# dV and the weight gradients stored from SyncE instead of GpSimd, in the backward pass of a decode layer

## The chip, the cores and the metric

The kernel runs on one core of a Trainium2 chip. The metric is the device time of one execution in microseconds (us), the median of several runs. A profile is one more execution under the hardware profiler; its span is the time from the first to the last event, 1712.4 us for the kernel before.

A core has five engines, each with an instruction stream of its own that is worked through in order: TensorE (PE; PEld is its weight load), VectorE (DVE), ScalarE (ACT), GpSimd (POOL) and SyncE (SP). Data moves between device memory and the on-chip buffer by DMA. An engine issues a transfer with one instruction and goes on; 16 DMA engines carry it. Which engine issued a transfer decides the queue it stands in: q1 is SyncE's, q10 ScalarE's, q0 GpSimd's.

## The reference

One token per sequence for four sequences, 32 heads of 128, a cache of 4096 keys and values per head; then a gated MLP. The function returns the output and the gradients of its inputs. What matters here:

```python
q = (layernorm(x) @ wq)                              # (4, 32, 1, 128)
scores = einsum("bhqd,bhkd->bhqk", q, k_cache) * 128 ** -0.5
p = softmax(scores)
o = einsum("bhqk,bhkd->bhqd", p, v_cache)
h = x + o.reshape(4, 1, 4096) @ wo
gate, up = layernorm(h) @ w1, layernorm(h) @ w3
h2 = h + (silu(gate) * up) @ w2
# outputs: h2, and the vjp for grad_out of x, k_cache, v_cache, wq, wo, w1, w3, w2
```

With one query, the gradients of the caches are outer products. For each of the 128 (sequence, head) pairs, dV[k, :] = p[k] * dO[:] and dK[k, :] = dS[k] * q[:], where dS = p * (dP - c) * scale, dP[k] = V[k, :] . dO, and c is one number per pair. So each pair reads 1 MB of K once, 1 MB of V twice (forward and backward), and writes 1 MB of dK and 1 MB of dV, all bf16. The weight gradients are outer products too, some 13 MB in all.

## The kernel before

The kernel has a forward part (0 to about 650 us), a short middle part with the MLP, and a backward part from about 700 us to the end. All large buffers are taken from 23 equal slots of 8 KB per partition, handed out and given back in the order of a queue:

```python
free = deque(range(NSLOT))              # NSLOT = 23
class Slot:
    def __init__(self, name, src=free):
        self.i = src.popleft()
        self.t = slotp.tile([P, SLOT], BF16, name=name, tag=f"slot{self.i}")
    def give(self):
        free.append(self.i)
```

`give` is bookkeeping while the program is built. When a slot is used again, the instruction that writes it waits on the chip until its last reader, a store for instance, has finished.

The backward part loads each head's V into a ring of seven slots, transposes it in place (TensorE to PSUM, ScalarE back), and stores two outer products per head. L770 is VectorE's multiply in `outer`, L781 the dV store, L797 the V load and L1201 the dK store:

```python
def V_T(s, ps, part=range(SJ // GW)):
    ...
    for g in part:                                          # 4 parts of 8 transposes
        pt = ps.tile([P, GW, P], BF16, tag="tps", name="pt_tps")
        for i in range(GW):
            nc.tensor.transpose(pt[:, i, :], v[:, g * GW + i, :], ident_b[:])     # L764
        nc.scalar.copy(out=v[:, g * GW:(g + 1) * GW, :], in_=pt[:])               # L765

def grad_V(s):
    b, h = bh_of(s)
    gv = Slot("gv")
    outer(gv.heads(), P2s.pop(s), reps["rdo", s // REP][:, s % REP, :])           # L770
    nc.gpsimd.dma_start(out=rows_of(out_3[b, h]), in_=gv.heads())                 # L781
    if s > 1:
        gv.give()
    else:
        first_gv.append(gv)

def load_V2(eng=nc.sync):
    s = nv["next"]
    if s < NH:
        V2s[s] = Slot("V2", vring if vring else free)
        eng.dma_start(out=V2s[s].heads(), in_=cache_head(A_v_cache, s))           # L797
        nv["next"] += 1

def grad_K(s):
    b, h = bh_of(s)
    gk = Slot("gk")
    outer(gk.heads(), dS2s[s // B][:, s % B], reps["rq", s // REP][:, s % REP, :])  # L770
    nc.sync.dma_start(out=rows_of(out_2[b, h]), in_=gk.heads())                   # L1201
    gk.give()
```

`front(s)` transposes one head's V, makes dP with matmuls whose stationary operand is a small zero-padded window `zd` that GpSimd fills, and after every fourth head ScalarE copies dP out (dPr) and TensorE transposes it (dPT). `group_dS` makes dS of four heads on VectorE. GpSimd also doubles p into pairs for the outer product:

```python
def dO_window(s):                                            # GpSimd, L1142
    nc.gpsimd.tensor_copy(out=zd[s % B][:, 32:132:67], in_=dOT_bf[:, s:s + 1].to_broadcast([P, 2]))
def P_pairs(s):                                              # GpSimd, L1147
    nc.gpsimd.tensor_copy(out=P2s[s][:], in_=P_all[:, s, :, None].to_broadcast([P, SJ, 2]))

for s in range(2):
    dO_window(s)
for s in range(L):                                           # L = 5, LV = 3, S0 = 21, O0 = 2
    load_ahead(s); P_pairs(s); front(s)
    if s < 2: first_gv[s].give()
    elif s < LV + 1: grad_V(s)
group_dS(0)
for s in range(NH):                                          # NH = 128
    load_ahead(s + L)                                        # V loads: load_V2(nc.scalar)
    if s % REP == 0 and s + REP < NH: replicate(s + REP)     # rows of dO and q, for 4 heads
    P_pairs(s + L)
    if s + L < NH: front(s + L)
    ...
    if s > 0 and s + LV < NH: grad_V(s + LV)
    grad_K(s)
    if s % B == B - 1 and s + 1 < NH: group_dS((s + 1) // B)
    if s >= S0: step("s", 3 if s < S0 + 15 else 2)           # side work: dq, dx, weight gradients
    elif s >= O0: step("o")
step("s", 400)
```

The first two dV stores stand in the middle part, before the four `zd` windows are cleared (L1138). The side work makes the weight gradients in slots of their own and stores each from GpSimd: dwq four of 1 MB (L1026), dw2 two and dw1, dw3 two each of 0.9 MB (L1069, L1085), dwo four of 1 MB (L1096). It also loads wq (four of 1 MB) and w2 (two of 0.9 MB) again from SyncE.

Of the kernel before, what the change touches and what calls it, by code (L numbers as in the profile page):

```python
# [24 lines left out]
def kernel(  # L25
# [22 lines left out]
    nc = tc.nc  # L48
    P = nc.NUM_PARTITIONS
# [8 lines left out]
    HD = H * Dh  # L58
# [25 lines left out]
    def bh_of(s):  # L84
        return s % B, s // B

    def rows_of(ap):
        return ap.rearrange("(p j) d -> p j d", p=P)
# [89 lines left out]
    def ones_window(col):  # L178
# [11 lines left out]
                          in_=rowg[:, None, :, None].to_broadcast([P, 4, 8, 4]))  # L190
# [308 lines left out]
    def load_w2():  # L499
        sl = two_slots("w2")  # L500
        for i in range(2):
            nc.sync.dma_start(out=sl[i].b(7 * D).rearrange("p (c j) -> p c j", c=7),
                              in_=B_w2.rearrange("(p c) j -> p c j", c=FC)[:, i * 7:(i + 1) * 7, :])
        return sl
# [264 lines left out]
    def outer(dst, col2, row):  # L769
        nc.vector.tensor_tensor(  # L770
            out=dst.rearrange("p j (r t) -> p j r t", t=2),
            in0=col2[:, :, None, :].to_broadcast([P, SJ, Dh // 2, 2]),
            in1=row.rearrange("p (r t) -> p r t", t=2)[:, None, :, :].to_broadcast([P, SJ, Dh // 2, 2]),
            op=ALU.mult,
        )

    def grad_V(s):
        b, h = bh_of(s)
        gv = Slot("gv")
        outer(gv.heads(), P2s.pop(s), reps["rdo", s // REP][:, s % REP, :])  # L780
        nc.gpsimd.dma_start(out=rows_of(out_3[b, h]), in_=gv.heads())  # L781
        if s > 1:
            gv.give()
        else:
            first_gv.append(gv)
# [14 lines left out]
    with ExitStack() as cm:  # L800
# [108 lines left out]
        for b0, b1 in ((0, 1), (1, B)):  # L909
            ps = psA.tile([P, B, Dh], FP32, tag="rT", name="rep_ps")  # L910
            for b in range(b0, b1):
                for jj in range(DC):
                    nc.tensor.matmul(ps[:, b, :], lhsT=dhT[:, jj, b:b + 1].to_broadcast([P, P]), rhs=wo_page(0)[:, 0, jj, :],
                                     start=(jj == 0), stop=(jj == DC - 1))
            if b0 == 0:
                nc.vector.tensor_copy(out=rep_bufs["rdo"][0][:, 0:1], in_=ps[:, 0:1])
                grad_V(0)
            else:
                nc.scalar.copy(out=rep_bufs["rdo"][0][:, b0:b1], in_=ps[:, b0:b1])
        dO_columns(0, 8, psC, "cols")  # L920
        mid_w["wo"][0].give()
        grad_V(1)
        V_T(0, psT, range(2, SJ // GW))
        dO_rows(0, 8, psA, "rT")


    with ExitStack() as c2:
# [9 lines left out]
        def grad_flush():  # L937
            if gu:
                dst, ps, n = gu.pop()
                nc.scalar.copy(out=dst, in_=ps[:, 0:n])  # L940


        def grad_unit(dst, lhsT, rhs):
            n = rhs.shape[-1]
            ps = psg.tile([P, 512], FP32, tag="gps", name="gps")
            nc.tensor.matmul(ps[:, 0:n], lhsT=lhsT, rhs=rhs, start=True, stop=True)  # L946
            grad_flush()
            gu.append((dst, ps, n))


        def side_work():
# [65 lines left out]
            for cc in range(DC):  # L1017
                if cc == DC - 2:
                    w2 = load_w2()
                st = Slot("gwq")  # L1020
                for n8 in range(HD // 512):
                    grad_unit(st.b(HD)[:, n8 * 512:(n8 + 1) * 512], xhat_bf[0:B, cc * P:(cc + 1) * P],
                              flat.b(HD)[0:B, n8 * 512:(n8 + 1) * 512])
                    yield
                grad_flush()
                nc.gpsimd.dma_start(out=out_4[cc * P:(cc + 1) * P, :], in_=st.b(HD))  # L1026
                st.give()
            flat.give()
            fs.give()
# [32 lines left out]
            for i in range(2):  # L1062
                st = Slot("gw2")
                hw = hh_rows[:, i * 7 * P:(i + 1) * 7 * P].rearrange("b (p k) -> b k p", k=7)
                for k in range(7):
                    grad_unit(st.b(7 * D)[:, k * D:(k + 1) * D], hw[:, k, :], gr_bf)
                    yield
                grad_flush()
                nc.gpsimd.dma_start(out=out_8[i * 7 * P:(i + 1) * 7 * P, :].rearrange("(p c) j -> p c j", c=7),  # L1069
                                  in_=st.b(7 * D).rearrange("p (c j) -> p c j", c=7))  # L1070
                st.give()
            oflat = Slot("oflat")
# [2 lines left out]
            for (rows, out_ap) in ((dg_rows, out_6), (du_rows, out_7)):  # L1075
                for i in range(2):
                    st = Slot("gw13")
                    nw = hhat_bf[0:B, i * 2 * P:(i + 1) * 2 * P].rearrange("b (p k) -> b k p", k=2)
                    for k in range(2):
                        for (f0_, w_) in f_chunks:  # L1080
                            grad_unit(st.b(2 * F)[:, k * F + f0_:k * F + f0_ + w_],
                                      nw[:, k, :], rows[:, f0_:f0_ + w_])
                            yield
                    grad_flush()
                    nc.gpsimd.dma_start(out=out_ap[i * 2 * P:(i + 1) * 2 * P, :].rearrange("(p c) f -> p c f", c=2),  # L1085
                                      in_=st.b(2 * F).rearrange("p (c f) -> p c f", c=2))
                    st.give()
            r1.give()
            for h0 in range(0, H, 8):
                st = Slot("gwo")  # L1090
                ow = oflat.b(HD)[0:B, h0 * P:(h0 + 8) * P].rearrange("b (p k) -> b k p", k=8)
                for k in range(8):
                    grad_unit(st.b(8 * D)[:, k * D:(k + 1) * D], ow[:, k, :], dh_bf)
                    yield
                grad_flush()
                nc.gpsimd.dma_start(out=out_5[h0 * P:(h0 + 8) * P, :].rearrange("(p k) j -> p k j", k=8),  # L1096
                                  in_=st.b(8 * D).rearrange("p (k j) -> p k j", k=8))
                st.give()
            oflat.give()
            r2.give()  # L1100

        units["s"] = side_work()


# [113 lines left out]
        for s in range(L):  # L1218
            load_ahead(s)
            P_pairs(s)  # L1220
            front(s)
            if s < 2:
                first_gv[s].give()
            elif s < LV + 1:
                grad_V(s)
# [51 lines left out]
```

## Time and profile before

| | |
|---|---|
| time, median of 3 runs | 1716.86 us (1714.01 to 1718.6) |
| span of the profiled run | 1712.4 us |
| HBM read, written | 422.59 MB, 282.34 MB |
| mean rate over the span | 413 GB/s |
| busy: PE, DVE, ACT, POOL | 74%, 72%, 57%, 28% |

How to read it. The page gives busy time by engine, and then the span in 40 equal slices: a digit is the busy share of a slice in tenths, and two rows below give the busy share of the 16 DMA engines and the GB/s that they moved. A row of a DMA queue gives its packets, its MB and the time of its packets as a share of 16 engines' span. A row of a group of instructions reads: line, engine, operation, output <- input, count, then busy us and mean ns of one, then the idle time of the engine just before them and what ended most of it. A row of the waits reads: who waited, for whom, us in total, number of times, the longest. A row of a stretch reads: the stretch, its length, busy us and count for PE, PEld, DVE, ACT and POOL, then TensorE's granted clock, the DMA share and GB/s. A row of DMA issues gives output <- input, the issuing engine, count, size and the median us from issue to landing.

### The profile page before, as it was taken

To read this page: it belongs to the slowest core of one execution; us is meant where nothing else is said; L and a number is where in the kernel's file an instruction comes from. 1 tells how busy PE (TensorE), PEld (TensorE's weight loads), DVE (VectorE), ACT (ScalarE), POOL (GpSimd) and SP (SyncE) were. 2 spreads that over 40 slices of the span, in tenths; PEclk is the share of its full clock that TensorE was granted. 3 is DMA by queue.
4 is the path that set the end of the run, shared out by engine and by line. 5 is a ranking of instruction groups with operands and counts; after the bars stand their busy time and mean duration, and the time that the engine had idled before them with its cause. 6 is when DMAs were issued, how large, how long until landed. Compare 5 with 4: busy or idle time off the path is not lost. (4 is left out here: it accounts for less than half of the span.)

```text
span 1712.4 us, 38306 instructions
## 1 busy us (share of the span) xinstructions
PE 1259.2 (74%) x16180; PEld 930.6 (54%) x16180; DVE 1229.2 (72%) x1294; ACT 969.7 (57%) x1502; POOL 474.7 (28%) x822
## 2 busy tenths in 40 slices
PE   5889888888888888776788986675657656656660
PEld 4767677677677666644556764443334433333330
DVE  5989999989998996466667548475546465656584
ACT  3556445444544444676655466675766656666660
POOL 1211232223222321122333245353223231211140
PEclk8999999999999999898776579887896788887885
DMA  9999999999999999799999999999999999999997
GB/s 401 424 424 424 424 424 424 424 420 424 419 424 407 420 407 401 307 385 423 425 425 426 426 365 422 425 424 425 425 426 426 424 417 418 424 425 423 425 424 299
DMA packets 101740, 707.49 MB, mean 413 GB/s; under 512 B 11052, under 2 KB 15288, under 8 KB 17600
## 3 DMA queue, kind: packets, MB, share of 16 engines
q1 hardware_dynamic: 63568, 432.04, 60.5%
q0 software_dynamic: 20864, 148.22, 20.7%
q10 hardware_dynamic: 17136, 124.79, 17.6%
q8 instruction: 127, 2.08, 0.5%
q14 instruction: 45, 0.37, 0.1%
HBM read 422.59 MB, written 282.34 MB: 412 GB/s over the span
## 5 line engine op out<-in xcount | busy, mean ns | idle before, releaser
L765 ACT COPY V<-pt_tps 128x1024 bf16<-128x1024 bf16 x512 | 490.8, 1025 | 155.3 <-PE pt_tps L764 115.9
L764 PE MATMUL pt_tps<-ident_b,V 128*128 128x128 bf16 x4096 | 359.0, 249 | 206.5 <-ACT V L765 201.4
L764 PEld LDWEIGHTS <-V 128*128 128x128 bf16 x4096 | 306.8, 114 | 269.1 <-issue 257.8
L770 DVE TENSOR_TENSOR gv<-P,reps 128x4096 bf16<-128x4096 bf16 x125 | 287.0, 2296 | 129.4 <-DMA out_dram<-gv 123.6
L770 DVE TENSOR_TENSOR gk<-dS,reps 128x4096 bf16<-128x4096 bf16 x128 | 292.5, 2287 | 112.7 <-DMA out_dram<-gv 80.4
L421 DVE TENSOR_TENSOR PK<-Kn,PK 128x4096 bf16<-128x4096 bf16 x128 | 292.4, 2284 | 26.4 <-POOL PK L417 26.0
L436 PE MATMUL M_ps<-PK,Vn 128*128 128x130 bf16 x4096 | 285.8, 222 | 32.3 <-DMA Vn<-in_A_v_cache_dram 31.9
L436 PEld LDWEIGHTS <-Vn 128*128 128x128 bf16 x4096 | 253.8, 99 | 52.0 <-DMA Vn<-in_A_v_cache_dram 43.0
L328 DVE STREAM_TRANSPOSE KT<-Kn 128x512 f32<-128x512 f32 (+1 forms) x321 | 250.7, 797 | 0.3 <-issue 0.2
L1177 PE MATMUL dP_ps<-V,zd 128*32 128x512 bf16 x1024 | 185.3, 452 | 72.3 <-ACT V L765 61.8
L323 ACT COPY KT<-pt_tps 128x1024 bf16<-128x1024 bf16 x128 | 129.5, 1012 | 185.3 <-PE pt_tps L322 150.7
L781 POOL DMA_DIRECT2D out_dram<-gv x128 | 68.4, 535 | 498.9 <-DVE gv L770 470.6
L417 POOL COPY PK<-P_all 128x64 bf16<-128x64 bf16 x128 | 32.6, 255 | 415.5 <-ACT P_all L411 412.4
L334 POOL TENSOR_TENSOR W<-qrep,wmask 128x128 bf16<-128x128 bf16 x128 | 122.9, 960 | 83.0 <-PE S_ps L354 68.3
L1147 POOL COPY P<-P_all 128x64 bf16<-128x64 bf16 x127 | 137.3, 1081 | 0.0
L1177 PEld LDWEIGHTS <-zd 128*32 128x32 bf16 x1024 | 37.3, 96 | 161.8 <-issue 140.3
L1142 POOL COPY zd<-dOT_bf 128x2 bf16<-128x2 bf16 x128 | 90.5, 708 | 71.5 <-PE dP_ps L1177 71.5
L1191 DVE TENSOR_SCALAR dPr<-dPT_ps,c_rep 128x32 f32<-128x32 f32 x128 | 23.2, 242 | 119.1 <-PE dPT_ps L1159 118.9
L1131 ACT CAST reps<-rep_ps 128x512 bf16<-128x512 f32 x62 | 36.4, 586 | 121.0 <-DVE gk L770 86.5
L411 ACT COPY P_all<-pt_P 32x64 bf16<-32x64 bf16 x256 | 52.1, 203 | 53.8 <-PE pt_P L407 51.6
L322 PE MATMUL pt_tps<-ident_b,Kn 128*128 128x128 bf16 x1024 | 81.0, 224 | 0.0
L446 PE MATMUL kP_ps<-PK,onesw 128*32 128x512 bf16 x1024 | 79.9, 389 | 0.0
(244 smaller groups left out, 1358.7 us busy)
## 6 DMA issues: line engine op xcount, KB each, us to landing
Kn<-in_A_k_cache_dram SPq DMA_DIRECT2D x128, 1024.0 KB, 15.3
Vn<-in_A_v_cache_dram SPq DMA_DIRECT2D x128, 1024.0 KB, 15.6
out_dram<-gv POOLq DMA_DIRECT2D x128, 1024.0 KB, 29.7
out_dram<-gk SPq DMA_DIRECT2D x128, 1024.0 KB, 13.9
V<-in_A_v_cache_dram ACTq DMA_DIRECT2D x119, 1024.0 KB, 14.8
V<-in_A_v_cache_dram SPq DMA_DIRECT2D x9, 1024.0 KB, 18.3
wq<-in_A_wq_dram SPq DMA_DIRECT2D x8, 1024.0 KB, 18.3
out_dram<-gw POOLq DMA_DIRECT2D x6, 896.0 KB, 42.0
```

Source lines behind the costliest of these rows:

```text
L322: nc.tensor.transpose(pt[:, i, :], Kn[:, c * GW + i, :], ident_b[:])
L323: nc.scalar.copy(out=KT[:, c * GW:(c + 1) * GW, :], in_=pt[:])
L328: nc.vector.transpose(out=KT[:, c * w_:(c + n) * w_], in_=Kn[:, c * w_:(c + n) * w_])
L334: nc.gpsimd.tensor_tensor(out=W[:, hl], in0=qrep[:, :, s:s + 1].to_broadcast([P, 4, 32]), in1=wmask[:, hl, None, :].to_broadcast([P, 4, 32 ...
L421: nc.vector.tensor_tensor(out=PK[:, :, 0:Dh].rearrange("p j (r t) -> p j r t", t=2), in0=Ks[s].heads().rearrange("p j (r t) -> p j r t", t=2),
L436: nc.tensor.matmul(hold["M"][:], lhsT=Vn[:, j, :], rhs=PK[:, j, :], start=(j == 0), stop=(j == SJ - 1))
L764: nc.tensor.transpose(pt[:, i, :], v[:, g * GW + i, :], ident_b[:])
L765: nc.scalar.copy(out=v[:, g * GW:(g + 1) * GW, :], in_=pt[:])
L770: nc.vector.tensor_tensor(out=dst.rearrange("p j (r t) -> p j r t", t=2), in0=col2[:, :, None, :].to_broadcast([P, SJ, Dh // 2, 2]), in1=r ...
L1142: nc.gpsimd.tensor_copy(out=zd[s % B][:, 32:132:67], in_=dOT_bf[:, s:s + 1].to_broadcast([P, 2]))
L1147: nc.gpsimd.tensor_copy(out=P2s[s][:], in_=P_all[:, s, :, None].to_broadcast([P, SJ, 2]))
L1177: nc.tensor.matmul(rows["acc"][32 * c:32 * (c + 1), :], lhsT=zq_window(zd[hl], 2 * hl + u), rhs=VT[:, j0:j0 + 4, :], start=(hl == 0 and u ...
```

## The change

All large stores that GpSimd issued are issued by SyncE: the 128 stores of dV and the 14 of the weight gradients. The dK stores were SyncE's and the V loads of the backward loop ScalarE's already, so with the change no large transfer is left to GpSimd; it keeps a few of some kilobytes. The purpose is to free GpSimd of issuing and of waiting for VectorE, and to have the stores in a queue of the hardware's own descriptor generation. Five lines change, each in the same way:

```diff
@@ grad_V @@
         outer(gv.heads(), P2s.pop(s), reps["rdo", s // REP][:, s % REP, :])
-        nc.gpsimd.dma_start(out=rows_of(out_3[b, h]), in_=gv.heads())
+        nc.sync.dma_start(out=rows_of(out_3[b, h]), in_=gv.heads())
@@ side_work: dwq @@
-                nc.gpsimd.dma_start(out=out_4[cc * P:(cc + 1) * P, :], in_=st.b(HD))
+                nc.sync.dma_start(out=out_4[cc * P:(cc + 1) * P, :], in_=st.b(HD))
@@ side_work: dw2 @@
-                nc.gpsimd.dma_start(out=out_8[i * 7 * P:(i + 1) * 7 * P, :].rearrange(...),
+                nc.sync.dma_start(out=out_8[i * 7 * P:(i + 1) * 7 * P, :].rearrange(...),
@@ side_work: dw1, dw3 @@
-                    nc.gpsimd.dma_start(out=out_ap[i * 2 * P:(i + 1) * 2 * P, :].rearrange(...),
+                    nc.sync.dma_start(out=out_ap[i * 2 * P:(i + 1) * 2 * P, :].rearrange(...),
@@ side_work: dwo @@
-                nc.gpsimd.dma_start(out=out_5[h0 * P:(h0 + 8) * P, :].rearrange(...),
+                nc.sync.dma_start(out=out_5[h0 * P:(h0 + 8) * P, :].rearrange(...),
```

The order of instructions on TensorE, VectorE and ScalarE stays as it was. SyncE's stream gets the dV stores between the dK stores, in the order in which VectorE makes them. In the built program, the large transfers of SyncE and ScalarE wait on semaphores of one set, those of GpSimd on semaphores of another:

```
before, SyncE:   dK store   [waits DMAHW2, DVE]      after, SyncE:   dV store   [waits DMAHW0, DVE]
                 dK store   [waits DMAHW6, DVE]                      dK store   [waits DMAHW1, DVE]
before, GpSimd:  dV store   [waits DMASW5, DVE]                      dV store   [waits DMAHW2, DVE]
before, ScalarE: V load     [waits DMAHW4, ACT]      after, ScalarE: V load     [waits DMAHW0, ACT]
```

More of the change, by code (lines that the diff above doesn't have):

```diff
@@ L1068, in side_work @@
                 grad_flush()
-                nc.gpsimd.dma_start(out=out_8[i * 7 * P:(i + 1) * 7 * P, :].rearrange("(p c) j -> p c j", c=7),
+                nc.sync.dma_start(out=out_8[i * 7 * P:(i + 1) * 7 * P, :].rearrange("(p c) j -> p c j", c=7),
                                   in_=st.b(7 * D).rearrange("p (c j) -> p c j", c=7))
@@ L1084, in side_work @@
                     grad_flush()
-                    nc.gpsimd.dma_start(out=out_ap[i * 2 * P:(i + 1) * 2 * P, :].rearrange("(p c) f -> p c f", c=2),
+                    nc.sync.dma_start(out=out_ap[i * 2 * P:(i + 1) * 2 * P, :].rearrange("(p c) f -> p c f", c=2),
                                       in_=st.b(2 * F).rearrange("p (c f) -> p c f", c=2))
@@ L1095, in side_work @@
                 grad_flush()
-                nc.gpsimd.dma_start(out=out_5[h0 * P:(h0 + 8) * P, :].rearrange("(p k) j -> p k j", k=8),
+                nc.sync.dma_start(out=out_5[h0 * P:(h0 + 8) * P, :].rearrange("(p k) j -> p k j", k=8),
                                   in_=st.b(8 * D).rearrange("p (k j) -> p k j", k=8))
```

## The prediction

> **What bounds the kernel now.** I read the page first, its row of slices and its queues. Four rows carry the reading: the busy share of the DMA engines and their GB/s in 40 slices of 42.8 us, and the three queues that carry the large transfers (q1 is SyncE's, q10 ScalarE's, q0 GpSimd's).
>
> ```profile
> DMA  9999999999999999799999999999999999999997
> GB/s 401 424 424 424 424 424 424 424 420 424 419 424 407 420 407 401 307 385 423 425 425 426 426 365 422 425 424 425 425 426 426 424 417 418 424 425 423 425 424 299
> ...
> q1 hardware_dynamic: 63568, 432.04, 60.5%
> q0 software_dynamic: 20864, 148.22, 20.7%
> q10 hardware_dynamic: 17136, 124.79, 17.6%
> ```
>
> The reader is to see that nearly every slice stands at one rate, 424 GB/s, whichever queues are at work: slices 1 to 7 hold loads of SyncE alone, the later ones loads and stores of three queues. The kernel is bound by its DMA. Then I cut the span where the slices dip, and asked for busy time and DMA of each stretch (the last two columns are the DMA share and GB/s):
>
> ```profile
> 700.00:740.00 40.00, 27.11 (x317) 17.84 (x315) 21.07 (x17) 26.82 (x31) 10.56 (x29) 0.91 0.73 275
> 740.00:1000.00 260.00, 209.51 (x1915) 154.34 (x1910) 159.09 (x119) 155.02 (x177) 76.98 (x101) 0.75 1.01 425
> 1000.00:1020.00 20.00, 14.38 (x160) 10.13 (x158) 18.31 (x14) 14.30 (x17) 16.02 (x14) 0.89 0.81 299
> 1020.00:1695.00 675.00, 418.89 (x4040) 265.00 (x4037) 418.50 (x298) 429.24 (x533) 201.82 (x274) 0.82 1.01 424
> 1695.00:1712.40 17.40, 0.00 (x0) 0.00 (x0) 0.00 (x0) 0.00 (x0) 0.00 (x0) 0.50 0.27 116
> ```
>
> All 707.49 MB at 424 GB/s would take 1668.6 us. The span is 1712.4, so 43.8 us are lost. Each stretch loses its length times (1 - its GB/s / 424): 700 to 740 us 14.1, 1000 to 1020 us 5.9, the end 12.6. What is left, 11.2 us, lies before 700 us, where the change moves nothing: the first dV store is issued at 702.4. So the change can reach 14.1 + 5.9 + 12.6 = 32.6 us at the very most.
>
> Last I read the waits and the issues, to see who waits for the stores that move:
>
> ```profile
> L781 POOL DMA_DIRECT2D out_dram<-gv x128 | 68.4, 535 | 498.9 <-DVE gv L770 470.6
> ...
> out_dram<-gv POOLq DMA_DIRECT2D x128, 1024.0 KB, 29.7
> out_dram<-gk SPq DMA_DIRECT2D x128, 1024.0 KB, 13.9
> V<-in_A_v_cache_dram ACTq DMA_DIRECT2D x119, 1024.0 KB, 14.8
> ```
>
> ```profile
> DVE gv L770 <- DMA out_dram<-gv: 123.6, 42, 6.8
> DVE dPr L1191 <- PE dPT_ps L1159: 118.9, 11, 22.9
> DVE gk L770 <- DMA out_dram<-gv: 80.4, 30, 9.5
> ```
>
> A dV store lands 29.7 us after its issue, a dK store after 13.9, and VectorE waits 123.6 + 80.4 = 204 us for slots that a dV store still holds. That looks like 204 us to gain. It isn't: during these waits the DMA engines are full (the 424 GB/s rows), so VectorE waits for bytes, not for a slow queue.
>
> **What the Trainium skill says.** "DMA: Bandwidth & Descriptors", section "Issuing engines are not separate DMA queues": transfers of any issuing engine run on the same 16 DMA engines and interleave. The trace agrees: share divided by MB is 0.140% for q1, 0.140% for q0, 0.141% for q10, so a byte costs the same on each. The same page, "Queues, rings and completion order": a DMA engine takes turns among the queues that hold work. The trace fits; three queues that all want the engines divide them evenly, and GpSimd's, with more stores pending, has the longest time to landing. Its section "Latency and other measured facts" gives about 1 us to the first byte for GpSimd's path and 0.6 us for the other; the trace shows no such gain, for the shortest dV landing is 4.2 us and the shortest dK landing 4.7. "SBUF — State Buffer", section "SBUF: two separate sides", warns that VectorE can lock GpSimd out while it writes descriptors and leave the DMA engines idle. No full stretch here shows it: they are at 424 with or without q0.
>
> **The change part by part.**
>
> Bytes: none added or removed. At equal cost per byte the 1668.6 us stay: 0 us.
>
> GpSimd's issues: 128 + 14 large stores at 0.53 us, some 76 us of an engine that is 28% busy. It also stands still 470.6 us behind VectorE in these issues, and its small copies (zd, P) stand behind them in program order. Where DMA is full that costs nothing. In the dip at 700 to 740 us it does: no store can flow until the chain of V transposes for the first five heads is through, and the first dP matmul waits 3.52 us, until 706.48, for a zd copy. GpSimd had stood at the issue of the second dV store until 704.94. Without it the cast (0.22 us) can start when the c_ps matmuls end, near 703.0, then the four memsets (0.67) and the zd copy (0.2): 704.1 or so. Gain about 2.2 us, on the path.
>
> SyncE's issues: 142 more at 0.33 us, 47 us on an engine that does nothing else. 0 us.
>
> Semaphores: the built program shows something that the diff doesn't. Large transfers of SyncE and ScalarE take eight semaphores in turn, in program order, and each waits for the transfer that had it eight before; GpSimd's have eight of their own. In the kernel before, dV stores stood outside; now a head has three transfers in one ring of eight (V load, dV store, dK store), and the side work's join them. A V load then waits for the dV store of about three heads earlier, and that wait is in ScalarE's own instruction stream, ahead of its copies. In flight before, between 1020 and 1640 us: dV 77 x 36.2 / 620 = 4.5, dK 77 x 13.7 / 620 = 1.7, V 78 x 14.6 / 620 = 1.8, side work about 1.1, together 9 MB (an estimate, from median landings). After, at most 8, or 8 x 2.47 = 19.8 us of work (1.0486 MB at 424 GB/s is 2.47 us). That still fills the engines, if nobody holds the ring longer. Per head the DMA needs 3 x 2.47 = 7.4 us, ScalarE 429.24 / 78 = 5.5, VectorE 418.5 / 80 = 5.2, so each can follow. When the dV store lands on which ScalarE waited, about seven stores are still to go, some 17 us; ScalarE and TensorE need about 5 us to the next dS and VectorE 3.5 to the next store, 8.5 in all. The ring is closed with some 8 us to spare: 0 us in the mean. In the dip at 1000 us, where ScalarE needs 12 us for a head (its V loads are issued at 991.7 and 1003.5), a held ring may cost about 2 us more.
>
> The end: VectorE stops at 1688.9, all 16 engines are busy to about 1696, and then the rows fall to 27 GB/s, a sixteenth of 424, for some 8 us: one DMA engine finishes alone. Fewer stores in flight and one order for all may shorten this by 2 or 3 us; I count 2.
>
> Sum: -2.2 (first dip) + 2 (second) - 2 (end) = -2.2 us from 1716.86. As the slot order also becomes the landing order, which may trim small waits, I set 1713.
>
> **The rivals.**
>
> First rival, GpSimd's queue was the brake: its descriptors cost the DMA engines time, or make the one engine fall behind that ends last. For it: dV landings of 29.7 us against 13.9, and the lone engine at the end. Against it: equal cost per byte, and the same 424 in stretches without q0. If the lone engine is its doing, 8 us go at the end: about 1703. It can't exceed the 32.6 us.
>
> Second rival, the ring of eight becomes a new wait: ScalarE stands at a V load, TensorE and VectorE stall behind it, and the DMA engines run dry in places that are full today because nine transfers and a separate dV queue bridge a stall. For it: VectorE already has stalls of up to 22.9 us at dPr, and ScalarE already waits for dK stores ahead of its V loads:
>
> ```profile
> ACT V L765 <- DMA out_dram<-gk: 17.9, 7, 5.8
> ```
>
> Against it: the 8 us to spare above, and that slots bound the stores in flight before semaphores do at 740 to 1000 us. If one group of four heads in three among the last 20 groups lost 3 us, that is 20 us: 1735.
>
> Third rival, the changed order on SyncE: weight loads now stand behind dV stores too. But a slot of a load comes from the oldest store, which lands first now; I give it nothing.
>
> **Range and chances.** The hidden case (nothing but a few us) has about two thirds, around 1713; the first rival a sixth, down to 1703; the ring a sixth, up to 1735 and thinly beyond. Range 1700 to 1735. Faster by over 2% means under 1682.5, a gain of 34 us, more than all the idle time that the change can reach: 0.01. Slower by over 2% means over 1751, a ring that runs dry often: 0.09. Within 2%: 0.90.
>
> **What would show it.** Right: about 424 GB/s in all slices from 18 to 38 but the dip; the first dP matmul near 704 us; dV and dK landings alike near 20 us; VectorE's wait for stores moved from one name to the other and about as long in total; GpSimd's 470 us gone and nothing gained by it. First rival: share per MB falls, or the last 17 us shrink to under 10. Second: new slices under 410 between 740 and 1690 us, with ScalarE waiting for gv or gk stores ahead of its V loads by far more than today's 18 us. I'd be wrong most likely by a stall that I took for bridged.

## The result and the profile after

The changed kernel takes 1728.3 us (median of four runs, 1727.0 to 1731.4) against 1716.7: a ratio of 1.0071, 95% interval 1.0051 to 1.0091. It is slower by 0.7%, 15 us above the 1713 that was predicted, inside the range: a loss of 12 us where a gain of 4 was forecast. The profiled span went from 1712.4 to 1727.6 us, by 15.2; the ledger below is of these two executions.

First the page of the kernel after: the DMA share and GB/s in 40 slices, the packets, and the two queues that are left for large transfers.

```profile
DMA  9999999999999999799999989999999999999998
GB/s 402 423 425 423 425 423 425 423 425 423 415 423 409 423 406 401 280 425 420 418 419 369 395 341 418 423 416 418 417 423 420 414 412 421 420 413 414 413 425 354
DMA packets 101741, 707.50 MB, mean 410 GB/s; under 512 B 11052, under 2 KB 15288, under 8 KB 17600
...
q1 hardware_dynamic: 84016, 580.16, 80.8%
q10 hardware_dynamic: 17136, 124.79, 17.9%
```

The bytes are the same. Counted from 0, slices 0 to 15 are as before but for a few GB/s, and 16 and 17 are the first dip, which the wider slices cut elsewhere. From slice 18 on, two things have changed. Slices 21 to 23 are low (369, 395, 341, where one slice dipped before). And most slices after them stand at 412 to 421 where most stood at 422 to 426, although their digit is a 9 as before. The second sign is easy to overlook: a DMA engine that is full isn't yet at its rate.

The stretches of the backward part, cut where the slices change (columns: busy us of TensorE, its weight loads, VectorE, ScalarE and GpSimd; the share of its full clock that TensorE was granted, DMA share, GB/s). The kernel after:

```profile
700.00:740.00 40.00, 28.26 (x330) 18.68 (x329) 21.44 (x17) 27.27 (x32) 11.79 (x24) 0.91 0.76 288
740.00:900.00 160.00, 112.79 (x1151) 78.41 (x1151) 102.17 (x76) 102.33 (x119) 26.94 (x45) 0.82 1.01 421
900.00:1020.00 120.00, 106.44 (x782) 85.07 (x781) 62.20 (x49) 55.49 (x64) 29.85 (x27) 0.61 0.91 365
1020.00:1710.00 690.00, 445.01 (x4160) 287.26 (x4158) 427.04 (x304) 442.40 (x545) 285.47 (x180) 0.79 1.01 418
1710.00:1727.60 17.60, 0.00 (x0) 0.00 (x0) 2.16 (x1) 0.00 (x0) 0.00 (x0) 0.50 0.59 249
```

And the kernel before, in the two of these that the prediction didn't cut so:

```profile
740.00:900.00 160.00, 119.13 (x1238) 82.31 (x1234) 106.27 (x84) 107.44 (x125) 49.08 (x70) 0.83 1.01 425
900.00:1020.00 120.00, 104.75 (x837) 82.16 (x835) 71.13 (x49) 61.88 (x70) 43.92 (x45) 0.66 0.98 404
```

The prediction's measure, length times (1 - GB/s / 424), gives the loss of each stretch:

| stretch | lost before, us | lost after, us | difference |
|---|---|---|---|
| 700 to 740 | 14.1 | 12.8 | -1.3 |
| 740 to 900 | -0.4 | 1.1 | +1.5 |
| 900 to 1020 | 5.7 | 16.7 | +11.0 |
| 1020 to the end of the full part | 0 | 9.8 | +9.8 |
| the end | 12.6 | 7.3 | -5.3 |

The sum is 15.7, against 15.2 in the span. The same difference splits in a second way. Share of all queues times span is the time that packets took on a mean DMA engine: before 99.4% of 1712.4, or 1702.1 us; after 99.3% of 1727.6, or 1715.5. So 13.4 us are longer packets for the same bytes, and only some 2 are more idle time. The idle time hides two opposite moves: in 900 to 1020 the share fell from 0.98 to 0.91 (about 8 us more), and at the two ends idle time fell by about 6. I call 1702.1 and 1715.5 the packet time from here on. It is a sum of printed shares, each rounded to 0.1%, so it is good to about 3 us; the packet records added up one by one give 1699.4 and 1713.3 us, 13.9 apart.

The large groups that the change touches, in the page of the kernel after (GpSimd's copies of P first; then the issues, with the median us from issue to landing):

```profile
L1147 POOL COPY P<-P_all 128x64 bf16<-128x64 bf16 x127 | 218.6, 1721 | 346.2 <-DVE gv L770 345.8
...
out_dram<-gv SPq DMA_DIRECT2D x128, 1024.0 KB, 18.7
out_dram<-gk SPq DMA_DIRECT2D x128, 1024.0 KB, 18.8
V<-in_A_v_cache_dram ACTq DMA_DIRECT2D x119, 1024.0 KB, 10.2
```

dV and dK stores now land alike, near the 20 us of a ring of eight. V loads land in 10.2 us, earlier than the 14.8 of before. GpSimd's wait in the issues is gone, and most of it has only moved to its next copy. Last the waits (total us, times, longest):

```profile
DVE dPr L1191 <- PE dPT_ps L1159: 332.4, 28, 18.6
...
ACT V L765 <- DMA out_dram<-gv: 101.4, 22, 7.8
...
ACT V L765 <- DMA out_dram<-gk: 22.6, 3, 13.7
...
DVE gv L770 <- DMA out_dram<-gv: 10.7, 10, 2.3
...
DVE gk L770 <- DMA out_dram<-gv: 5.9, 5, 2.4
```

The wait for stores has changed engine. VectorE waited 204 us for slots that dV stores held; now 16.6 us (10.7 + 5.9), and 39.1 for stores of both kinds (22.5 us behind dK stores). ScalarE waited 17.9 us for stores ahead of its V loads; now 124.0 (101.4 + 22.6). The view books this wait at L765, the copy that comes next in ScalarE's stream. Behind ScalarE stand TensorE's V transposes, dP and dPT, and behind those VectorE, which now waits 332.4 us at dPr instead of 118.9.

### The profile page after: what moved, and what is told of

It is laid out like the page before. It is cut to its first block, busy times and chain, and to the rows that moved or that the text cites. A ratio compares the mean times of both kernels' runs of the same rounds, so it can differ in the third digit from the quotient of the medians.

```text
span 1727.6 us, 38312 instructions
## 1 busy us (share of the span) xinstructions
PE 1280.1 (74%) x16180; PEld 951.4 (55%) x16180; DVE 1227.7 (71%) x1294; ACT 971.6 (56%) x1502; POOL 523.6 (30%) x680
## 3 DMA queue, kind: packets, MB, share of 16 engines
q1 hardware_dynamic: 84016, 580.16, 80.8%
q10 hardware_dynamic: 17136, 124.79, 17.9%
## 5 line engine op out<-in xcount | busy, mean ns | idle before, releaser
L765 ACT COPY V<-pt_tps 128x1024 bf16<-128x1024 bf16 x512 | 491.5, 1024 | 248.5 <-PE pt_tps L764 117.5
L764 PE MATMUL pt_tps<-ident_b,V 128*128 128x128 bf16 x4096 | 374.2, 255 | 206.5 <-ACT V L765 201.2
L764 PEld LDWEIGHTS <-V 128*128 128x128 bf16 x4096 | 320.5, 117 | 266.1 <-issue 256.7
L1147 POOL COPY P<-P_all 128x64 bf16<-128x64 bf16 x127 | 218.6, 1721 | 346.2 <-DVE gv L770 345.8
L770 DVE TENSOR_TENSOR gv<-P,reps 128x4096 bf16<-128x4096 bf16 x125 | 287.9, 2303 | 21.1 <-DMA out_dram<-gv 10.7
L1191 DVE TENSOR_SCALAR dPr<-dPT_ps,c_rep 128x32 f32<-128x32 f32 x128 | 23.3, 245 | 332.4 <-PE dPT_ps L1159 332.4
L1142 POOL COPY zd<-dOT_bf 128x2 bf16<-128x2 bf16 x128 | 132.1, 1032 | 186.2 <-PE dP_ps L1177 186.2
L322 PEld LDWEIGHTS <-Kn 128*128 128x128 bf16 x1024 | 61.8, 99 | 25.7 <-issue 25.6
L400 ACT ACTIVATE Pn<-E,rl 128x1024 bf16<-128x1024 f32 x64 | 73.7, 1152 | 3.2 <-DVE rl L397 3.2
## 6 DMA issues: line engine op xcount, KB each, us to landing
out_dram<-gv SPq DMA_DIRECT2D x128, 1024.0 KB, 18.7
V<-in_A_v_cache_dram ACTq DMA_DIRECT2D x119, 1024.0 KB, 10.2
out_dram<-gw SPq DMA_DIRECT2D x6, 896.0 KB, 14.8
```

Source lines behind the costliest of these rows:

```text
L322: nc.tensor.transpose(pt[:, i, :], Kn[:, c * GW + i, :], ident_b[:])
L770: nc.vector.tensor_tensor(out=dst.rearrange("p j (r t) -> p j r t", t=2), in0=col2[:, :, None, :].to_broadcast([P, SJ, Dh // 2, 2]), in1=r ...
```

## The experiments

Two theories stood at the start. The **ring theory**: a V load waits in ScalarE's own stream for the store eight transfers earlier, the chain behind ScalarE stalls, and the DMA runs dry or out of step. The **queue theory**, a rival: what matters is which queues the bytes are in, and how they share the DMA engines, whatever ScalarE waits for. A third, that SyncE's long list of issues or the order of its loads costs something, stood beside them. All kernels compute the whole of the reference. Each ratio, with its 95% interval, is to the kernel before as it ran beside that kernel. There its median was 1714.3 to 1716.7 us, so medians of different experiments compare to about 2 us.

**dV alone** (the changed kernel, with the weight gradients back on GpSimd) and **weight gradients alone** (the kernel before, with these on SyncE):

```diff
# dv_only, against the kernel after: dwq, dw2, dw1 and dw3, dwo (dV stays on SyncE)
-                nc.sync.dma_start(out=out_4[cc * P:(cc + 1) * P, :], in_=st.b(HD))
+                nc.gpsimd.dma_start(out=out_4[cc * P:(cc + 1) * P, :], in_=st.b(HD))
# wgrads_only, against the kernel before: the same four lines the other way (dV stays on GpSimd)
```

> The changed kernel with the 14 weight-gradient stores put back on GpSimd; only the dV stores stay on SyncE. If the ring of eight semaphores with three transfers per head is the cause, nearly all of the loss stays: 1725 to 1729 us, ScalarE waiting some 100 us for dV stores ahead of its V loads. If the weight gradients in SyncE's stream are the cause (they wait for ScalarE's copies and hold dV and dK stores behind them), it falls back to 1715 to 1719.

> The kernel before with only the 14 weight-gradient stores moved to SyncE; dV stays on GpSimd. Ring of eight: two transfers per head and a few more, so no new waits: 1715 to 1719. Weight gradients as the cause: 1725 to 1729.

Measured: dV alone 1736.3 us, 1.0121 (1.0107 to 1.0136). Weight gradients alone 1721.3 us, 1.0038 (1.0025 to 1.0050). The dV stores are the larger part, but the two parts don't add: with dV on SyncE, moving the 14 others as well makes the kernel 8 us faster; with dV on GpSimd, the same move costs some 6.5 us. I have no cause for that. The second run holds a surprise for the ring theory, in its waits:

```profile
DVE dPr L1191 <- PE dPT_ps L1159: 292.6, 26, 23.7
...
ACT V L765 <- DMA out_dram<-gk: 124.1, 19, 16.6
```

ScalarE waits as long for its V loads as in the kernel after, and VectorE nearly as long at dPr, at half the cost in time.

**V loads elsewhere.** In the kernel after, the V loads of the backward loop are issued from GpSimd, or from SyncE, so that nothing in ScalarE's stream waits for a transfer of the ring:

```diff
-                load_V2(nc.scalar)
+                load_V2(nc.gpsimd)      # v_gpsimd, in both places;  nc.sync in v_sync
```

> The changed kernel with the V loads of the backward loop issued from GpSimd, so that stores (SyncE) and loads (GpSimd) have eight semaphores each and ScalarE issues nothing. Ring theory: ScalarE never waits for a store, no dry stretch but that of the kernel before, 1708 to 1718. If stores from SyncE's queue are slow in themselves, or if loads and stores simply pack worse in two queues than in three: 1725 to 1730. If GpSimd's loads come late because GpSimd stands behind its small copies: TensorE waits for V, over 1730.

> The changed kernel with the V loads of the backward loop on SyncE too: one queue for all large transfers, ScalarE issues none and waits for no store. The ring of eight stays, and its order. First theory (ScalarE's waits at the V loads cost the time): back to 1716 to 1721, the waits of ScalarE for stores gone. Second theory (a queue that starts again after a pause stretches the packets under way; the V queue does it over 100 times in the changed kernel): packets over 400 ns nearly vanish, DMA at 424 GB/s where it is busy. Rival (the ring itself lets the DMA run dry, whoever waits at it): 1728 or more, since a V load that waits for its slot now holds the stores behind it as well.

Measured: from GpSimd 1718.7 us, 1.0014 (1.0004 to 1.0025). Its dip stays:

```profile
900.00:1020.00 120.00, 106.30 (x789) 83.77 (x788) 65.61 (x46) 57.47 (x66) 30.65 (x43) 0.61 0.94 384
```

ScalarE has no wait for a store ahead of its V copies here, and VectorE waits only 80.9 us at dPr, yet the DMA share falls to 0.94. GpSimd stands some 500 us in front of its V loads instead. So the dry stretch doesn't need a wait in ScalarE's stream; more on it below.

From SyncE, with every large transfer of the backward loop in one queue, 1714.4 us, 0.9994 (0.9988 to 1.0001): the time of the kernel before. The stretches of v_sync, with the columns as above:

```profile
900.00:1020.00 120.00, 105.62 (x806) 83.31 (x802) 66.39 (x46) 58.20 (x66) 36.78 (x29) 0.63 1.00 401
1020.00:1690.00 670.00, 420.69 (x4052) 265.84 (x4051) 424.75 (x299) 430.19 (x534) 169.09 (x175) 0.83 1.01 424
```

Its waits:

```profile
DVE gv L770 <- DMA out_dram<-gv: 113.1, 42, 5.2
...
DVE dPr L1191 <- PE dPT_ps L1159: 94.8, 10, 18.6
DVE gk L770 <- DMA out_dram<-gv: 86.0, 36, 7.0
```

This is the kernel after with one engine changed for the V loads, and both signs of the loss are gone: share 1.00 instead of 0.91 between 900 and 1020, 424 instead of 418 GB/s from 1020 on. What 401 GB/s at a share of 1.00 leaves there is long packets. VectorE's waits are back at 199 us for dV stores and 94.8 at dPr. So SyncE's issues cost nothing, even with 119 more of them, and freeing GpSimd brings next to nothing. What costs is V loads on ScalarE beside all stores on SyncE. That agrees with the ring theory, and with the queue theory as well, for the V loads' own queue is gone too.

**The wait without the stall.** In the kernel after, the V load is issued after `front`, so that ScalarE's copies for the transposes come ahead of the wait:

```diff
+        load_ahead(L)                  # ahead of the loop
         for s in range(NH):
-            load_ahead(s + L)
             ...
                 front(s + L)
+            load_ahead(s + L + 1)
```

> The changed kernel with each V load issued after the transposes of its iteration instead of before them. Same queues, same bytes, same eight semaphores; the load stands one head looser in the ring and ScalarE's copies come before the wait. Ring theory: ScalarE's waits for dV stores ahead of its copies fall from 101 us to under 30, the stretch at 920 to 1020 us gets most of its 12 us of idle DMA back, time 1716 to 1721. If the hardware queue of SyncE is slower in itself than GpSimd's for these stores: unchanged, 1727 to 1730.

Measured: 1729.4 us, 1.0086 (1.0073 to 1.0099), no better than the kernel after. One of its waits:

```profile
ACT V L765 <- DMA out_dram<-gv: 12.6, 2, 7.4
```

The wait ahead of the transposes' copies shrank from 124.0 to 12.6 us, and part of it moved to ScalarE's copies for the weight gradients (13.1 us in the largest of these rows). All waits of ScalarE for transfers add up to 84 us (after 141, before 39). VectorE still waits 317 us at dPr. The ring theory in the form "ScalarE's stall at the V load makes the loss" missed here; between 900 and 1020 us the share is 0.93, against 0.91. The kernel still has the loads on ScalarE, waiting in its stream; only what stands behind them differs.

**dK from GpSimd**, the kernel after with the roles of dK and dV exchanged: the load on of three queues as in the kernel before.

```diff
-            nc.sync.dma_start(out=rows_of(out_2[b, h]), in_=gk.heads())
+            nc.gpsimd.dma_start(out=rows_of(out_2[b, h]), in_=gk.heads())
```

> The changed kernel with the dK stores moved to GpSimd: dV and weight gradients from SyncE, dK from GpSimd, V from ScalarE. Three queues and two large transfers per head in the ring, as in the kernel before, with the roles of dV and dK exchanged. Ring theory and theory of the pauses: 1715 to 1723 (some 4 us over the kernel before for the weight gradients, as measured alone). If it is the dV stores that don't suit SyncE's queue: 1727 or more.

Measured: 1720.2 us, 1.0024 (1.0014 to 1.0034). Its waits:

```profile
DVE dPr L1191 <- PE dPT_ps L1159: 256.1, 26, 17.6
ACT V L765 <- DMA out_dram<-gv: 123.6, 17, 16.6
```

After wgrads_only, this is the second kernel in which ScalarE waits 124 us and VectorE over 250 at dPr; only 4 us are lost. The length of these waits doesn't measure the loss.

**More transfers in the ring.** Each dV store is cut in two of 512 KB, first in the kernel after (four transfers of a head in the ring), later in v_sync, where ScalarE has no part in it:

```diff
-        nc.sync.dma_start(out=rows_of(out_3[b, h]), in_=gv.heads())
+        for j in range(0, SJ, SJ // 2):
+            nc.sync.dma_start(out=rows_of(out_3[b, h])[:, j:j + SJ // 2, :], in_=gv.heads()[:, j:j + SJ // 2, :])
```

> The changed kernel with each dV store cut in two of 0.5 MB, both from SyncE: four transfers per head in the ring of eight, so it holds two heads instead of 2.7. Ring theory: the waits grow, 1740 to 1790, with dry stretches through the whole backward part. If the ring is not what costs: 1727 to 1732, the bytes are the same and half a megabyte with rows of 4 KB is little slower.

> All large transfers from SyncE, with each dV store cut in two: the shorter ring, but ScalarE waits at none of it. If what costs is that ScalarE waits for the ring in its own stream: within 4 us of the uncut kernel with V loads from SyncE, 1713 to 1719, where the same cut cost 8.5 us with the loads on ScalarE. If a shorter ring, or rows of 4 KB, cost by themselves: 1721 to 1727.

Measured: 1736.9 us, 1.0119 (1.0098 to 1.0141) for the first, 8.5 us above the kernel after; 1735.6 us, 1.0104 (1.0083 to 1.0124) for the second, about 20 us above v_sync. The first by itself looks like the ring theory at work, in its direction if not its size. The second shows as large a loss without ScalarE. Its ScalarE has no wait for a store ahead of its V copies, VectorE's wait at dPr is 86.6 us, and the DMA is full in the long stretch:

```profile
1020.00:1690.00 670.00, 418.78 (x4004) 265.86 (x4003) 410.06 (x290) 425.19 (x529) 161.26 (x170) 0.82 1.01 405
```

A share of 1.01 and 405 GB/s: packets took longer, with no engine dry. Two things show in the packet records. The pieces move in packets of 4 KB, which take 159 ns where half an 8 KB packet is 154.5 (309 / 2); 31,423 of them between 745 us and the end make 8.8 us per DMA engine. And more of the 8 KB packets are stretched (1118 against 392 over 400 ns, 18 us more in all). The smaller pieces cost that without any wait of ScalarE for the ring, so the first run tells little of such waits. A ring of eight also holds fewer bytes when some of its transfers are half as large; whether that or the pieces themselves stretch the other packets is not separated here.

**The dry stretch.** Between 900 and 1020 us TensorE is busy for 106 of 120 us at a granted clock of 0.61; the float32 matmuls of the side work for dq (dq_ps) are 37 of these 106. The next edit does two pieces of side work in each of the first 15 heads instead of three, in the kernel after, in v_sync and in the kernel before:

```diff
-                step("s", 3 if s < S0 + 15 else 2)
+                step("s", 2)
```

> The changed kernel with two units of side work per head from the start, where it has three for the first 15 heads. The dq matmuls in fp32 (0.22 us each, nine per head) become six per head, so TensorE's head time in that stretch falls from about 10 us to about 8.5. If the idle DMA at 920 to 1020 us comes from a compute chain of over 7.4 us a head: the dry stretch shrinks from some 12 us of idle to under 6, time 1720 to 1724. If it comes from the ring alone: unchanged within 2 us.

> All large transfers from SyncE, and two units of side work per head from the start. The even side work took 7 us off the changed kernel; with V loads on SyncE only the dry stretch of the kernel before is left to take, some 4 us of idle at 980 to 1020 us: 1709 to 1712. If the dry stretch has already gone with ScalarE's waits: 1713 to 1716.

> The kernel before with two units of side work per head from the start, nothing else. It has the same dry stretch at 1000 us, 4 us of idle: 1709 to 1713, if the stretch vanishes and the side work, which ends some eight heads later, doesn't reach the end of the kernel. Otherwise 1714 to 1717.

Measured: in the kernel after (even_side) 1720.9 us, 1.0022 (1.0007 to 1.0037), 7 to 8 us less. Its stretch:

```profile
900.00:1020.00 120.00, 99.93 (x835) 76.84 (x835) 75.62 (x52) 66.17 (x74) 42.84 (x31) 0.70 1.00 411
```

And two of its waits:

```profile
ACT V L765 <- DMA out_dram<-gv: 92.7, 20, 8.9
...
ACT V L765 <- DMA out_dram<-gk: 37.9, 7, 8.8
```

The share is back at 1.00 while ScalarE still waits 131 us for stores ahead of its V loads (92.7 + 37.9) and VectorE 303 at dPr. So the idle DMA between 900 and 1020 is worth about 7 us. It is TensorE that sets the pace there. Of ScalarE's waits for stores at L765 in the kernel after, 14.6 us lie between 740 and 900 us and 109.4 after 1020; between 900 and 1020 there is none, and TensorE is never held up by a load. What the earlier waits take away is the lead of the computation over the stores. By 900 us ScalarE had copied back the transposes of 28.2 heads in the kernel after and of 29.2 before, with as many stores landed (25 of dV and 22 of dK in both). The kernels with three pieces of side work fall in this order: 30.0 heads and shares of 1.00 and 1.01 (v_sync, v_sync_halves), 29.2 and 0.98 (before, wgrads_only), 29.0 and 0.96 or 0.94 (dk_gpsimd, v_gpsimd), 28.0 to 28.5 and 0.91 to 0.93 (after, dv_only, v_after_front, dv_halves). even_side had no more lead, 28.0 heads, but TensorE did 15.2 heads in the stretch for the 12.8 of the kernel after. The rate there is still 411 GB/s at a share of 1.00: the packets stay long. In v_sync the edit gives 1711.9 us, 0.9976 (0.9966 to 0.9986), the only kernel clearly faster than the kernel before:

```profile
900.00:1020.00 120.00, 97.73 (x916) 73.87 (x916) 81.70 (x55) 70.16 (x79) 25.54 (x34) 0.84 1.01 426
1020.00:1690.00 670.00, 393.94 (x3927) 255.63 (x3926) 412.26 (x290) 416.15 (x519) 132.59 (x168) 0.83 1.01 423
```

In the kernel before it gives nothing, 1714.9 us, 1.0004 (0.9992 to 1.0017; its 13 runs reach from 1713.7 to 1721.8, so the median alone flatters it): 900 to 1020 rose to 424 GB/s, and 1020 to 1690 fell from 424 to 420.

**The kernel before with V loads on SyncE** and even side work; dV stays on GpSimd:

```diff
-                load_V2(nc.scalar)      # in both places
+                load_V2(nc.sync)
-                step("s", 3 if s < S0 + 15 else 2)
+                step("s", 2)
```

> The kernel before with V loads from SyncE and even side work; dV and weight gradients stay on GpSimd. ScalarE's 39 us of waits at the V loads go as well, but the DMA is full there: 1709 to 1713, the same as with V loads on ScalarE. If they cost something: 1704 to 1708.

Measured: 1740.8 us, 1.0144 (1.0127 to 1.0161), the slowest of all, where a gain was expected. Its long stretch, and the queues of its page:

```profile
1020.00:1690.00 670.00, 418.34 (x3917) 270.00 (x3913) 386.74 (x279) 414.70 (x516) 214.61 (x266) 0.79 1.01 405
```

```profile
q1 hardware_dynamic: 80704, 556.83, 78.0%
q0 software_dynamic: 20864, 148.22, 21.0%
```

ScalarE waits for no store ahead of its V copies, the DMA engines are full, and they move 405 GB/s. It differs from v_sync_even by the dV and weight-gradient stores on GpSimd alone, and that is worth 29 us here. Beside V loads on ScalarE, the same stores on GpSimd are 12 us better than on SyncE. So in these runs no single queue is the slow one: the combination counts.

**All of it in one table.** Packet time (shares of all queues times span, as above) stands beside the profiled span; the last two columns are from the packet records of the trace. Span, packet time and packets are of one profiled execution of each kernel, which isn't always near the median: dv_only's was 5 us faster. A packet of 8 KB takes 309 ns as a rule, and some take far longer; in the kernel after, 422 of the 954 long ones took 550 to 670 ns. Between 745 us and 30 us before the end, the 8 KB packets over 400 ns are counted, and the time above 309 ns of all 8 KB packets is added up, per DMA engine. The 4 KB packets of dv_halves and v_sync_halves are not in these two columns.

| kernel | median, us | span | packet time | over 400 ns | excess, us |
|---|---|---|---|---|---|
| v_sync_even | 1711.9 | 1710.5 | 1701.9 | 257 | 7.3 |
| before | 1716.7 | 1712.4 | 1702.1 | 362 | 8.5 |
| v_sync | 1714.4 | 1714.5 | 1705.9 | 392 | 10.8 |
| before_even | 1714.9 | 1711.6 | 1704.8 | 533 | 12.0 |
| dk_gpsimd | 1720.2 | 1717.2 | 1706.9 | 669 | 13.9 |
| wgrads_only | 1721.3 | 1719.5 | 1707.5 | 687 | 16.2 |
| v_gpsimd | 1718.7 | 1720.2 | 1709.9 | 717 | 15.9 |
| even_side | 1720.9 | 1716.2 | 1712.8 | 865 | 18.7 |
| after | 1728.3 | 1727.6 | 1715.5 | 954 | 20.9 |
| dv_only | 1736.3 | 1729.2 | 1715.4 | 939 | 22.0 |
| v_after_front | 1729.4 | 1723.0 | 1714.4 | 1039 | 21.8 |
| dv_halves | 1736.9 | 1738.4 | 1728.0 | 1033 | 23.6 |
| v_sync_halves | 1735.6 | 1735.2 | 1735.2 | 1118 | 28.9 |
| before_v_sync_even | 1740.8 | 1743.1 | 1734.4 | 2077 | 42.1 |

Packet time spreads over 33 us, the rest of the span (span minus packet time) over 0 to 14. Span minus excess is 1698 to 1715 in every row, 1707 in the kernel after. As an account this is settled: most of what separates these kernels is stretched packets. As a cause it is not, for it doesn't say what stretches them.

One thought was that a queue that pauses and starts again does it. In the kernel after, the V queue starts again after more than 0.3 us without a packet 102 times (37 before), and 367 of the 550 long store packets lie from 0.7 us ahead of such a start to 1.0 us after one, in 18% of the time. It fits that kernel and falls on others: v_sync and v_sync_halves, with one queue, have no such pause and 392 and 1118 long packets, and in before_v_sync_even only 10 of 726 long packets of q0 and 380 of 1351 of q1 lie near one of the 81 starts of q0.

One thing holds in all fourteen kernels: the surplus of long packets lies where loads and stores are under way together. After the last load has landed, 0 to 5 of some 1300 to 3700 packets of 8 KB are long. In the forward part (20 to 640 us), loads alone, 174 to 199 of some 31,500 are, about 0.6%, hardly different from kernel to kernel. From 745 us to the last load it is 0.6% in v_sync_even, 0.8% in the kernel before, 2.1% in the kernel after and 4.5% in before_v_sync_even. This says where the stretching is and not what does it.

## Why the prediction was right in range and 15 us off

**What bounds the kernel: right.** DMA is the limit in all fourteen kernels: 1702 to 1735 us of packet time in 1711 to 1743 us. That gains are small by nature held as well; the best one gains 4 us.

**GpSimd's issues: right, 1.3 us for 2.2.** The first dP matmul, from its instruction row (start, duration, idle time before it):

```profile
705.17 1.05 PE L1177 MATMUL dP_ps<-V,zd 128*32 128x512 bf16 x8 [2.53 <-POOL zd L1142]
```

It starts at 705.17 instead of 706.48; 704.1 was predicted. The cast ahead of the zd copy took 1.68 us in the kernel after for the 0.22 I had allowed.

**SyncE's issues: right, 0 us.** v_sync has every one of them, and 119 V loads on top, at the time of the kernel before.

**The end: right in direction.** It lost 7.3 us instead of 12.6, so 5 were gained for the 2 that I counted. It is no sign of the first rival, though: the gain is in the tail alone, and with GpSimd's queue gone the packet time rose. (The 1703 of that rival doesn't follow from its own terms: 8 us in place of the 2 counted for the end would have given about 1707.)

**Semaphores: the mechanism was named and its term mis-sized.** The step read "The ring is closed with some 8 us to spare: 0 us in the mean", and for the dip "about 2 us more". The stretch around that dip took 11.0 us instead, some 8 of them idle DMA and 3 longer packets. The 8 us to spare came from durations of ScalarE, TensorE and VectorE averaged over 1020 to 1690 us. Between 900 and 1020 TensorE was already busy for 105 of 120 us and set the pace. The ring wasn't held in the dip, as that step had it, but before it: 14.6 us of waits from 740 to 900 us, and at 900 us one head less of lead (28.2 for 29.2), which a TensorE without free time can't win back. One head is 7.4 us of DMA by the prediction's own sum, near the 8 that ran idle. even_side, which takes some of that work away, brings the share back to 1.00. The second rival's sign was there as well: three slices at 369, 395 and 341, and ScalarE's wait at V loads from 17.9 to 124.0 us. But its reading of this wait, time lost wherever ScalarE stands, failed: in those slices ScalarE waits for no store, and dk_gpsimd and wgrads_only have the same 124 us and lose 4 and 6.5.

**VectorE's wait: wrong.** "Moved from one name to the other and about as long in total" did not hold: of the 204 us behind dV stores, 39.1 behind stores of both kinds are left. The wait became one for the chain behind ScalarE; with dPr added it is 323 us before (204 + 118.9) and 371.5 after (39.1 + 332.4).

**Bytes: the step that failed.** "At equal cost per byte the 1668.6 us stay: 0 us." In the kernel before, q1, q0 and q10 did cost the same per byte, and from that I took that a byte costs the same in any arrangement of queues. I also leaned on the Trainium skill, "DMA: Bandwidth & Descriptors", section "Issuing engines are not separate DMA queues", by which transfers interleave on the same 16 DMA engines whatever engine issues them, and issuing from several engines at once saves only the time to issue. They do interleave, but the measurement differs on the price: after and v_sync differ by the issuing engine of V loads alone, and by 9.6 us of packet time, before_v_sync_even and v_sync_even by the issuing engine of the stores, and by 32.5. Equal cost inside one kernel says that the queues share whatever cost there is, not that the cost is fixed. In the kernel after, q10's 124.79 MB took 17.9% of 1727.6 us, 2.48 us per MB, against 17.6% of 1712.4, 2.42, before: the shares hardly differ, the times do. Nor is the cost equal any more: q1's 580.16 MB took 2.41 us per MB. My own list of signs had "about 424 GB/s in all slices"; it would have caught this, but nothing in the sum had a term for it.

So of the 15.2 us, about 13 were in the term "bytes: 0", about 8 in the term for the ring, and some 6 came back at the two ends. That 1728 lies in the range is in part luck: the range reached to 1735 for a ring that leaves the DMA idle, and most of the loss came as longer packets, which no rival foresaw. With V loads on SyncE the time is near the forecast, 1714.4 for 1713, but no run shows that this is so for the prediction's reasons.

**What stays open:** what stretches the packets when loads and stores share the engines, and why the weight gradients' place counts with the opposite sign depending on where dV is stored. By the runs it is none of these alone: the length of ScalarE's waits, the number of issues on an engine, a restart of a queue, the use of GpSimd's queue. Nor is it how much is under way: added up from the issue and the landing of every large transfer, a mean of 9.2 MB (of 2^20 bytes) was in flight from 1020 to 1680 us before, 6.6 after, 7.9 in v_sync and 9.8 in before_v_sync_even, which has the most long packets.

## What to carry to other kernels

When a kernel is bound by DMA, compare the time that packets take for the same bytes (share times span), in each stretch, and not the busy share alone: 1.01 stood beside 405 and beside 426 GB/s. Before a transfer moves to another queue, look in the built program for semaphores that it will share with a transfer in a compute engine's stream, and size that wait by stage, not from the mean: what lead does it take from the computation before a stretch in which the computation sets the pace? Here all large transfers of the backward loop on the engine that computes nothing, with the side work spread evenly, was the best arrangement (1711.9 us), and half of that move was worse than none.

## What the runs showed of the hardware

- Full DMA engines don't have one rate: with the share at 1.01 in 1020 to 1690 us they moved 424 GB/s (before, v_sync), 420 (before_even) and 405 (v_sync_halves, before_v_sync_even), for the same bytes in the whole kernel.
- A packet of 8 KB takes 309 ns or, in 257 to 2077 of some 47,000 cases in the backward part of a kernel with whole stores, over 400 ns. With only stores in flight, after the last load, at most 5 were that long in any kernel.
- Storing dV in pieces of 512 KB, with rows half as long, cost about 20 us in a one-queue kernel (1714.4 to 1735.6), though the DMA engines stayed full between 1020 and 1690 us: some 9 us of packet time are the 4 KB packets themselves (159 ns each), and the 8 KB packets took 18 us more.
- A single V queue beside one queue of stores lets loads land in 10.2 us and stores in 18.7; in one queue together all three land in 20 (19.7, 20.0 and 20.0). This fits the turns among queues that the prediction quotes.
